# Seven-product second layers on 256-column blocks, one batch behind the first layers; first layers back to one level

## The chip, the cores and the metric

The kernel runs on one core of a Trainium2 chip. The metric is device time in microseconds (us): 1341.12 us, the median of three runs (1341.06 to 1343.45). "PE" is the matrix engine (TensorE), "PEld" its weight loads, "DVE" the vector engine, "ACT" the scalar engine, "POOL" GpSimd and "SP" the engine that issues the transfers.

## The reference, cut to what matters

Attention with a threshold mask gives `x` of 1152 tokens by 512. Two mixtures of experts follow, the first with 8 experts and gates from a normalisation, the second with 4 experts and given gates:

```
for e in range(E):
    h = np.maximum(x @ w1[e], 0.0)          # 1152x512 @ 512x1024
    out += P[:, e:e + 1] * (h @ w2[e])      # 1152x1024 @ 1024x512
```

Nearly all of the arithmetic is in these two matrix products per expert. All data are fp32.

## The kernel before

Every fp32 operand of a matmul is kept as two fp32r tiles, a high part (`hi`) and what it leaves over (`lo`), and a product is three passes: lo by hi, hi by lo and hi by hi. `split` (L70) makes the pair: ACT casts the high part (L72), POOL or DVE subtracts (L77).

Attention and part of experts 0 and 1 come first (up to some 330 us). Then follow 22 half experts, each with 512 of an expert's 1024 hidden columns (`halves`, L622): two of expert 0 with one batch of 576 tokens, twelve of experts 2 to 7, and eight of the second mixture. A batch is `c` = 0 or 1; 64 tokens of each are the "tail", which is gathered into a ninth token tile.

A first layer (`x @ w1`) of one batch is done in seven products for eight (Winograd's form of Strassen's method): tokens in two halves of 288, inputs and hidden columns in two halves, so that a product is 2 groups `g` of 6 matmuls with 288 columns (`layer1`, L929, 14 slots). The sums of weights are made on POOL, those of x beforehand. Sixteen of the 22 half experts, the set `TWO`, take both batches jointly and apply the same trick once more inside products 2 and 7 (`layer1_two`, L1049): 162 matmuls instead of 168.

A second layer (`layer2`, L1256) is plain: nine token tiles, each 4 hidden blocks by 3 passes by 512 output columns, so 108 matmuls. DVE then adds each tile times its gate to `acc` (L1284).

Each engine works its own list of instructions strictly in the order in which the program writes them. The weights of the next half expert are cooked (sum on POOL, cast on ACT, subtraction on POOL) from generators that `tick` (L763) advances between groups of matmuls, at most every second tick and `LAG` ticks after the sum they need. PSUM has 8 banks. After the last half expert of the first mixture (`turn`), `next_x` (L1201) turns the finished `acc` into the new x: PE transposes, ACT copies, and `pair` (L1243) makes the four sums and four splits on POOL.

Of the kernel before, what the change touches and what calls it, by code (L numbers as in the profile page):

```python
# [19 lines left out]
E1, E2 = 8, 4  # L20
# [10 lines left out]
def attention_two_moe_kernel(ctx, tc, qP, kP, qT, kT, vp, tau, wg, w1, w1s, w2, dp, m2w1s, m2w2, out):  # L31
# [495 lines left out]
    with ExitStack() as att:  # L527
# [76 lines left out]
        while raws:  # L604
# [11 lines left out]
    UNITS = (1, 2, 6, 7, 5, 3, 4)  # L616
    SLOTS = ((1, 0), (1, 1), (2, 0), (2, 1), (6, 0), (6, 1), (7, 0), (5, 0), (7, 1), (5, 1), (3, 0), (4, 0), (3, 1),
             (4, 1))
    HF = FT // 2
    ORDER = (2, 3, 0, 1)  # L620
    NB1, NB2 = 7, 5
    halves = [dict(w1=w1s, w2=w2, e=e, hf=h, chunks=(1,), p=p1) for e in (0,) for h in range(2)]  # L622
    halves += [dict(w1=w1s, w2=w2, e=e, hf=h, chunks=(0, 1), p=p1) for e in range(2, E1) for h in range(2)]
    turn = len(halves) - 1
    halves[turn]["chunks"] = (1, 0)
    halves += [dict(w1=m2w1s, w2=m2w2, e=e, hf=h, chunks=(0, 1), p=p2) for e in range(E2) for h in range(2)]
    halves[turn + 1]["chunks"] = (1, 0)
    TWO = {*range(3, turn), *range(turn + 3, len(halves))}
    base = [0]
    for i in range(len(halves)):  # L630
        base.append(base[-1] + (9 if i in TWO else 7))

    class Psum:
        def __init__(self):
            self.all = pool(ctx, "psum", 1, space=PSUM, reuse_waits="tile").tile([P, 8, 512], F32, name="mm")
            self.free, self.of = list(range(8)), {}

        def tile(self, *a, **kw):
            k = self.free.pop(0)
            t = self.all[:, k]  # L640
            self.of[id(t)] = t, (k,)
            return t
# [7 lines left out]

        def give(self, t):
            self.free.extend(self.of.pop(id(t))[1])

# [5 lines left out]
    shared = [xp.tile([P, 4608], F32, tag="shared", name="sums"), 0]  # L659

    def new_xy():
        if shared[0].dtype != F32:
            shared[0] = xp.tile([P, 4608], F32, tag="shared", name="sums")
# [8 lines left out]
    def cook1():  # L672


        def total(a, b, op):
            s = w1p.tile([P, DM], F32, tag="sum1", name="ws", bufs=3)
            G.tensor_tensor(s, a, b, op=op)
            return s, clock[0] + LAG

        for i, hv in enumerate(halves):  # L680
            a11, a12, a21, a22 = (w1p.tile([P, DM], F32, tag="raw1", name="raw", bufs=4) for _ in range(4))
            for k, a in enumerate((a11, a12, a21, a22)):
                nc.sync.dma_start(a, hv["w1"][hv["e"], hv["hf"], k])
            ready = clock[0] + LAND
            order = iter(range(base[i], base[i + 1]))

            def unit(src, at):
                yield next(order), at
                hi = w1p.tile([P, DM], F32R, tag="w1h", name="wh", bufs=NB1)
                lo = w1p.tile([P, DM], F32R, tag="w1l", name="wl", bufs=NB1)  # L690
                split(A, G, hi, lo, src)
                units[0].append((hi, lo))

            def within(src):
                x = w1p.tile([P, DM], F32, tag="sum1", name="wx", bufs=3)
                b = [src[:, k * P:(k + 1) * P] for k in range(4)]
                y = [x[:, k * P:(k + 1) * P] for k in range(4)]
                for k, (p, q, op) in enumerate(((b[2], b[3], ALU.add), (y[0], b[0], ALU.subtract),
                                                (b[0], b[2], ALU.subtract), (b[1], y[1], ALU.subtract))):
                    G.tensor_tensor(y[k], p, q, op=op)  # L700
                return x, clock[0] + LAG

            if i in TWO:
                yield 0, ready + LAG
                x2 = within(a12)
                yield from unit(a12, ready)
                yield from unit(*x2)
            yield 0, ready
            s1 = total(a21, a22, ALU.add)
            yield 0, ready  # L710
            s2 = total(s1[0], a11, ALU.subtract)
            yield from unit(a11, ready)
            if i not in TWO:
                yield from unit(a12, ready)
            yield 0, ready
            G.tensor_tensor(a21, a11, a21, op=ALU.subtract)  # L716
            s3 = a21, clock[0] + LAG
            yield 0, ready
            G.tensor_tensor(a12, a12, s2[0], op=ALU.subtract)
            s4 = a12, clock[0] + LAG  # L720
            if i in TWO:
                yield 0, ready
                x7 = within(a21)
                rest = s2, s1, s3, x7, s4
            else:
                rest = s2, s3, s1, s4
            for src in rest:
                yield from unit(*src)
            yield from unit(a22, ready)

    def cook2(w2p):
        raw = []
        todo2 = [(hv, k) for hv in halves for k in ORDER]
        for i in range(len(todo2)):
            while len(raw) < 3 and todo2:
                hv, k = todo2.pop(0)
                raw.append((w2p.tile([P, DM], F32, tag="raw2", name="raw", bufs=3), clock[0] + LAND))
                nc.sync.dma_start(raw[-1][0], hv["w2"][hv["e"], :, hv["hf"] * HF + k])
            yield i, raw[0][1]
            hi = w2p.tile([P, DM], F32R, tag="w2h", name="wh", bufs=NB2)  # L740
            lo = w2p.tile([P, DM], F32R, tag="w2l", name="wl", bufs=NB2)
            split(A, G, hi, lo, raw.pop(0)[0])
            units[1].append((hi, lo))

    cooks, heads = [cook1(), None], [None, None]
    heads[0] = next(cooks[0])

    def advance(k):
        heads[k] = next(cooks[k], None)

    def may(k):
        if cooks[k] is None or heads[k] is None:
            return False
        return heads[k][0] < freed[k] + (NB1, NB2)[k] and clock[0] >= heads[k][1]
# [8 lines left out]
    def tick(n=1):  # L763

        clock[0] += 1
        first = [k for k in (0, 1) if heads[k] is not None and clock[0] >= last[0] + PACE]
        first.sort(key=lambda k: 2 * (bisect(base, len(units[0])) - 1 if k == 0 else len(units[1]) // HF) + k)
        for k in first:
            if may(k):
                advance(k)  # L770
                last[0] = clock[0]
                break
        for _ in range(n):
            while behind and next(behind[0], None) is None:
                behind.pop(0)

    def need(k, u):
        while len(units[k]) <= u:
            advance(k)
        return units[k][u]  # L780


    def gate():
        lt = shared[0][:2 * E1, 12 * HS:]
# [48 lines left out]
        give(norms)  # L833
        yield 1
# [72 lines left out]
    w2p = pool(ctx, "w2", reuse_waits="tile")  # L907
    cooks[1] = cook2(w2p)
    advance(1)
# [17 lines left out]
    turned = []  # L927

    def layer1(i, c):  # L929
# [3 lines left out]
        last = c == hv["chunks"][-1]  # L933
        side = [[hp.tile([P, HF, HS], F32R, tag=f"h{s}{k}", name="hs") for k in "hl"] for s in "lr"]
        tail = hv.setdefault("tail", None) or [hp.tile([P, HF, P], F32R, tag=f"t{k}", name="ht") for k in "hl"]
        hv["tail"] = tail
        hv.setdefault("side", {})[c] = side
# [7 lines left out]
        def done(src, s, k, to=None):  # L945

            hh, hl = (side[s][j][:, k] for j in range(2))
            A.activation(hh, src, AF.Relu)
            V.scalar_tensor_tensor(hl, src, 0.0, f(hh), op0=ALU.max, op1=ALU.subtract)  # L949
            if to is not None:  # L950
                give(to)

        def rest(s):

            q = (2 * c + s) * 32
            for j in range(2):
                G.tensor_scalar(tail[j][:, :, q:q + 32], f(side[s][j][:, :, 2 * P:]), 1.0, 1.0,  # L957
                                op0=ALU.mult, op1=ALU.mult)

        st, late = [{}, {}], [[], []]  # L960
        kept = {}
        for u, g in SLOTS:
            if u == 6 and not g:
                drain(i, c)
            if u == 2 and turned:
                next_x(turned.pop(0))
# [4 lines left out]
            if first:  # L971
                z[b] = bank()
# [397 lines left out]
```

## Time and profile before

| what | value |
|---|---|
| median of three runs | 1341.12 us |
| the profiled execution's own time | 1342.76 us |
| its span, first to last instruction | 1340.6 us |
| busy share of the span: PE, PEld, DVE, ACT, POOL | 98%, 86%, 53%, 45%, 59% |
| the chain that ended last, by engine | PE 86%, DVE 6%, ACT 4%, POOL 3% |
| its largest lines | L1276 39%, L1073 25%, L976 6% |

Matmuls overlap: one of 512 columns is shown as 0.39 us long, but the next starts some 0.23 us after it. What one costs is the distance from start to start. The mean duration of a group is not that distance.

### The profile page before, as it was taken

What the parts mean: (1) busy time and instruction counts of PE and PEld (TensorE: products, weight loads), DVE (VectorE), ACT (ScalarE), POOL (GpSimd) and SP (SyncE); (2) the same over time, 40 slices, a digit from 0 to 9 for tenths busy, and PEclk for the clock granted to TensorE, in tenths of its full rate; (3) what the DMA queues carried; (4) which work ended last, traced back from release to release, by engine and by line L of the source; (5) the groups of instructions that cost most, each with busy time, mean ns of one, the idle gap of its engine ahead of it and who ended that gap; (6) DMA issues with size and microseconds to landing.
All of it is one profiled execution on the core that took longest, in us unless ns stands there. A gap on an engine that the chain in (4) does not pass through costs nothing.

```text
span 1340.6 us, 20707 instructions
## 1 busy us (share of the span) xinstructions
PE 1310.9 (98%) x7681; PEld 1155.1 (86%) x7681; DVE 706.3 (53%) x1478; ACT 601.6 (45%) x1220; POOL 790.3 (59%) x997
## 2 busy tenths in 40 slices
PE   7998999999999999999999999999899999999998
PEld 4597988889888998899899889989789989988997
DVE  5799988356885443443444344344336344434434
ACT  6887786322443443343244334325534424433430
POOL 6886975342875646655564665554863656466540
PEclk9999999999999999999999999999999999999999
DMA  4542330010320221022022102211111201210202
GB/s 148 163 126 71 96 103 17 24 33 24 96 71 2 63 64 40 25 64 64 3 62 64 39 26 63 64 32 41 55 32 32 64 1 63 64 37 27 64 1 71
DMA packets 42052, 73.56 MB, mean 55 GB/s; under 512 B 5088, under 2 KB 10336, under 8 KB 41952
## 3 DMA queue, kind: packets, MB, share of 16 engines
q1 hardware_dynamic: 41664, 71.96, 18.1%
q8 instruction: 61, 1.00, 0.3%
q14 instruction: 39, 0.32, 0.1%
q10 hardware_dynamic: 288, 0.28, 0.1%
HBM read 69.86 MB, written 2.36 MB: 54 GB/s over the span
## 4 chain that ended last, share of the span: by engine, by line
PE 86%; DVE 6%; ACT 4%; POOL 3%; issue 1%; DMA 0%; POOLq 0%; DVEq 0%; ACTq 0%
PE mm L1276 39%; PE mm L1073 25%; PE mm L976 6%; PE mm L501 5%; PE mm L473 4%; PE sc L272 2%; PE pv L349 2%; DVE ex L296 1%; PE et L314 1%; DVE st L277 1%; ACT ex L292 1%; PE pv L358 1%; DVE etl L331 1%; PE pv L356 1%; ACT eth L321 0%
## 5 line engine op out<-in xcount | busy, mean ns | idle before, releaser
L77 POOL TENSOR_TENSOR wl<-raw,wh 128x512 fp32r<-128x512 f32 x198 | 257.6, 1308 | 380.9 <-ACT wh L72 374.3
L1276 PE MATMUL mm<-wh,hs 128*128 128x512 f32 x1344 | 433.7, 397 | 2.8 <-DVE hs L949 2.0
L1276 PEld LDWEIGHTS mm<-wh,hs 128*128 128x128 f32 x1344 | 252.3, 188 | 68.4 <-DVE hs L949 5.2
L1284 DVE SCALAR_TENSOR_TENSOR acc<-mm,p,acc 128x512 f32<-128x512 f32 x181 | 135.3, 749 | 271.6 <-PE mm L1276 271.5
L1276 PE MATMUL mm<-wl,hs 128*128 128x512 f32 x672 | 265.0, 394 | 0.0
L1276 PEld LDWEIGHTS mm<-wl,hs 128*128 128x128 f32 x672 | 126.3, 188 | 28.1
L72 ACT CAST wh<-raw 128x512 fp32r<-128x512 f32 x198 | 122.7, 624 | 38.3 <-POOL raw L716 24.2
L1109 ACT COPY A<-mm 128x288 f32<-128x288 f32 x32 | 12.9, 402 | 188.7 <-PE mm L1073 188.7
L1073 PE MATMUL mm<-xh,wl 128*128 128x288 f32 x432 | 96.5, 296 | 0.0
L1073 PE MATMUL mm<-xl,wh 128*128 128x288 f32 x432 | 96.4, 295 | 0.0
L1073 PE MATMUL mm<-xh,wh 128*128 128x288 f32 x432 | 96.2, 295 | 0.0
L1119 DVE SCALAR_TENSOR_TENSOR hs<-mm,hs 128x576 fp32r<-128x576 f32 x96 | 72.5, 755 | 33.7 <-ACT hs L1115 32.2
L1115 ACT ACTIVATE hs<-mm 128x576 fp32r<-128x576 f32 x96 | 62.5, 651 | 55.2 <-DVE mm L1112 48.8
L1073 PEld LDWEIGHTS mm<-xh,wl 128*128 128x128 f32 x432 | 70.8, 189 | 0.7
L1073 PEld LDWEIGHTS mm<-xl,wh 128*128 128x128 f32 x432 | 70.7, 189 | 0.8
L1073 PEld LDWEIGHTS mm<-xh,wh 128*128 128x128 f32 x432 | 71.0, 189 | 0.0
L306 POOL TENSOR_SCALAR ex<-ex,st 128x576 f32<-128x576 f32 x72 | 54.2, 753 | 26.5 <-DVE st L304 23.6
L1073 PE MATMUL mm<-xth,wl 128*128 128x288 f32 x304 | 69.0, 296 | 0.0
L1073 PE MATMUL mm<-xth,wh 128*128 128x288 f32 x304 | 68.9, 295 | 0.0
L1073 PE MATMUL mm<-xtl,wh 128*128 128x288 f32 x304 | 68.8, 295 | 0.0
L296 DVE SCALAR_TENSOR_TENSOR ex<-sc,st,ex 128x576 f32<-128x576 f32 x72 | 58.5, 813 | 14.8 <-ACT ex L292 10.8
L1276 PE MATMUL mm<-wh,ht 128*128 128x512 f32 x176 | 58.2, 392 | 1.8 <-POOL ht L957 1.8
(220 smaller groups left out, 2934.6 us busy)
## 6 DMA issues: line engine op xcount, KB each, us to landing
raw<-in_w SPq DMA_DIRECT2D x88, 256.0 KB, 3.0
raw<-in_w1s SPq DMA_DIRECT2D x56, 256.0 KB, 3.2
raw<-in_m2w1s SPq DMA_DIRECT2D x32, 256.0 KB, 2.8
raw<-in_m2w SPq DMA_DIRECT2D x32, 256.0 KB, 2.9
kr<-in_kT SPq DMA_DIRECT2D x22, 288.0 KB, 3.0
vr<-in_vp SPq DMA_DIRECT2D x24, 160.0 KB, 2.4
qr<-in_qT SPq DMA_DIRECT2D x8, 288.0 KB, 2.8
out_y<-acc SPq DMA_DIRECT2D x8, 256.0 KB, 2.0
```

The lines of the kernel that those rows point to most:

```text
L72: A.copy(hi, src)
L77: el.tensor_tensor(lo, src, f(hi), op=ALU.subtract)
L296: V.scalar_tensor_tensor(ex, u["sc"][:, :, :HS], st[:, 2:3], ex, op0=ALU.is_ge, op1=ALU.mult, accum_out=st[:, 3:4])
L306: G.tensor_scalar(exf, exf, st[:, 5:6], 1.0, op0=ALU.mult, op1=ALU.mult)
L473: T.matmul(ph[:, :n], lhsT=a[:, kt * P:(kt + 1) * P], rhs=x[:, kt, n0:n0 + n], start=i == 0 and kt == 0, stop=i == 2 and kt == KT - 1)
L501: T.matmul(py, lhsT=x, rhs=a, start=i == 0, stop=i == 3 * FT - 1)
L976: T.matmul(m, lhsT=w[:, (2 * g + kt) * P:(2 * g + kt + 1) * P], rhs=operand(u, kt, lo), start=first and j == 0, stop=j == len(ops) - 1, sk ...
L1073: T.matmul(m, lhsT=w, rhs=x, start=first and j == 0, stop=last and j == len(ops) - 1, skip_group_check=True)
L1115: A.activation(sides[c][s][0][:, k:k + 2], src, AF.Relu)
L1119: V.scalar_tensor_tensor(hl, src, 0.0, f(hh), op0=ALU.max, op1=ALU.subtract)
L1276: T.matmul(py, lhsT=hs[x][:, k, o:o + P], rhs=w, start=n == 0, stop=n == 3 * HF - 1)
L1284: V.scalar_tensor_tensor(acc[t], py, s, acc[t], op0=ALU.mult, op1=ALU.add)
```

## The change

- All first layers are done one batch at a time in seven products, in the order 1, 7, 6, 4, 5, 2, 3; `layer1_two` and the sums inside x (`within_x`) go.
- Nineteen second layers are also done in seven products, per batch: hidden columns in two halves, output columns in two halves of 256, tokens in two halves of 256. Each product is 2 slots of 6 matmuls with 256 columns. The tail tile is done in four plain pieces of 6. The three half experts in `PLAIN` keep the old form.
- The hidden values need sums of quadrants, each split into hi and lo, seven `places` per batch. `split_hidden` spreads that work over the next first layer: `push` makes one step of it per slot, `late(k)` holds a step until slot k of a first layer (k below 10), sum1, sum2 and sum4 are one DVE instruction each, `split_of` is an ACT cast and a DVE subtraction, and `mend` (ACT, then DVE) puts the difference of two quadrants into bank pair C; so the second layer of a batch runs after the first layer of the batch behind it. At `turn` and at the end the lag is closed.
- The weights are cooked from one list, `STEPS`, for both layers: per half expert 14 splits and 8 sums (before 9 + 4 splits, 4 sums and two sets of four small ones in a joint half expert).
- PSUM banks are handed out singly and in pairs; the second layer updates `acc` in 128x256 pieces, two per `quarter`.

```
-    UNITS = (1, 2, 6, 7, 5, 3, 4)
+    UNITS = (1, 7, 6, 4, 5, 2, 3)
+    PARTS = "22", "3", "2", "12", "1", "11", "4"
+    PLAIN = {0, 1, turn + 1}
-    LAND, LAG, PACE = 6, 4, 2
+    LAND, LAG, PACE = 8, 5, 2
...
+    STEPS = ((SUM, "s3", "a2", "a0", "a2", "-"), (SUM, "s2", "+", "a3", "s3", "-"), (UNIT, 0, "a0"),
+             (UNIT, 0, "s3", "s3"), (SUM, "s1", "a0", "s2", "a0", "+"), (UNIT, 0, "s2"), (UNIT, 0, "a3", "a3"),
+             (SUM, "s4", "s2", "a1", "s2", "-"), (UNIT, 0, "s1", "s1"), (UNIT, 0, "a1", "a1"),
+             (SUM, "t1", "+", "b3", "b2", "-"), (UNIT, 0, "s4", "s4"), (SUM, "t3", "b3", "b3", "b1", "-"),
+             (UNIT, 1, "b2", "b2"), (SUM, "t2", "+", "b1", "t1", "-"), (UNIT, 1, "t3", "t3"), (UNIT, 1, "t2"),
+             (UNIT, 1, "b0"), (SUM, "t4", "b0", "b0", "t2", "-", "t2"), (UNIT, 1, "t1", "t1"), (UNIT, 1, "t4", "t4"),
+             (UNIT, 1, "b1", "b1"))
...
+        k = max(len(agenda) - (0 if i - 1 in PLAIN else 2), 0)
+        agenda[k:k] = [(i, s) for s in steps[:2]]
+        agenda += [(i, s) for s in steps[2:]]
...
     def tick(n=1):
         clock[0] += 1
+        if agenda and clock[0] >= last[0] + (PACE if agenda[0][0] > 2 else 1) and ready_step():
+            advance()
+            last[0] = clock[0]
...
+    def slot(n=1):
+        for d in sorted((x for x in due if x[0] <= now[0]), key=lambda x: x[:2]):
+            due.remove(d)
+            d[2]()
+        push()
+        tick(n)
+        now[0] += 1
+        phase[1] += 1
...
     def layer1(i, c):
+        phase[:] = 1, 0
+        for n, u in enumerate(UNITS):
+            b = {7: "C", 4: "C", 2: "B"}.get(u, "A")
+            first = b not in ch
+            if first:
+                ch[b] = until(banks.pool.pair)
+            for g in range(2):
...
+                if g:
+                    m = wide(ch[b])
+                    if u in (1, 7, 6):
+                        v[u] = snap()
+                        A.copy(v[u], m)
+                    elif u == 4:
+                        V.tensor_tensor(m, v[6], m, op=ALU.add)
+                    if u == 4 and not plain:
+                        after(1, lambda m=m: A.activation(h21, m, AF.Relu))
+                    elif u == 5:
+                        h22 = ch["h22"] = v[7]
+                        V.tensor_tensor(h22, m, h22, op=ALU.add)
+                    if u == 5 and not plain:
+                        after(1, mend)
+                        after(2, lambda: whole(ch, "22", G, main(h22)))
+                    elif u == 2:
+                        V.tensor_tensor(m, v[1], m, op=ALU.add)
+                        work.append(split_hidden(ch))
+                slot()
...
+    def whole(ch, name, el, src):
+        hi, lo = ch["ops"][name] = until(place)
+        split(A, el, hi, lo, src)
+    def quadrant(ch, name, m, copy=None):
+        hi, lo = ch["ops"][name] = until(place)
+        A.activation(hi, main(m), AF.Relu)
+        if copy is not None:
+            A.activation(copy, main(m), AF.Relu)
+        A.activation(th, rest(m), AF.Relu)
+        V.scalar_tensor_tensor(lo, main(m), 0.0, f(hi), op0=ALU.max, op1=ALU.subtract)
+        V.scalar_tensor_tensor(tl, rest(m), 0.0, f(th), op0=ALU.max, op1=ALU.subtract)
...
+    def split_hidden(ch):
+        whole(ch, "3", V, main(ch["C"]))
+        order = ((upper_right, 0), (sum1, 1), (sum2, 2), (upper_left, 3), (lambda: split_of("1"), 5),
+                 (lambda: split_of("2"), 6), (sum4, 7), (lambda: split_of("4", 2), 9))
+        for step, k in order:
+            yield from late(k)
+            yield from step()
...
-    def layer2(i, c):
+    def layer2(ch):
+        for n, part_ in enumerate(PARTS):
+            if end and n == (i != turn):
+                tail_tile()
+            for k in range(2):
+                product(m[:, 256 * k:256 * k + 256], lambda j, kt: hi[j][:, kt, P * k:P * (k + 1)], 0, w,
+                        not k and part_ in ("22", "3", "12"))
+                if k:
+                    places.append(hi)
+                    if part_ in ("22", "2"):
+                        A.copy(v[part_], m)
+                    elif part_ == "12":
+                        V.tensor_tensor(BB, v["22"], BB, op=ALU.add)
+                        quarter(1, 0, BB, True)
+                    elif part_ == "11":
+                        V.tensor_tensor(CC, v["2"], CC, op=ALU.add)
+                        quarter(0, 0, CC, True)
...
+                if i == turn and turned and c == hv["chunks"][-1]:
+                    next_x(turned.pop(0))
+                slot(1 + (i == turn))
+        if i == turn:
+            turned.extend(4 * c + t for t in (2, 3, 0, 1))
...
+    for n, (i, c) in enumerate(chunks):
+        ch = layer1(i, c)
+        ready.append(ch)
+        while ready and (i in PLAIN or len(ready) > 1 or i == turn and c == 0):
+            (layer2_plain if i in PLAIN else layer2)(ready.pop(0))
+    for ch in ready:
+        layer2(ch)
```

## Rows read from the trace of the kernel before

**Rows 1.** The page: busy us (share of the span) and instructions of each engine.

```profile
PE 1310.9 (98%) x7681; PEld 1155.1 (86%) x7681; DVE 706.3 (53%) x1478; ACT 601.6 (45%) x1220; POOL 790.3 (59%) x997
```

**Rows 2.** Busy by stretch: length, PE, PEld, DVE, ACT, POOL (instructions), clock, DMA, GB/s.

```profile
600.00:700.00 100.00, 99.94 (x568) 88.67 (x567) 41.76 (x65) 37.71 (x69) 60.45 (x73) 1.00 0.15 43
800.00:900.00 100.00, 99.65 (x567) 88.43 (x566) 41.62 (x64) 35.71 (x66) 53.89 (x60) 1.00 0.19 53
900.00:1000.00 100.00, 94.85 (x563) 83.61 (x562) 41.35 (x81) 46.83 (x125) 66.50 (x84) 1.00 0.13 38
```

**Rows 3.** The chain in order of time: start us, us, what, instructions.

```profile
666.33 21.52 PE mm L1073 x162
...
687.88 25.36 PE mm L1276 x108
713.24 21.59 PE mm L1073 x162
```

**Rows 4.** PE in order of time, attention: start, us, line, op, tiles, shape.

```profile
134.93 0.63 PE L356 MATMUL pv<-etl,vhl 128*128 128x256 f32 x4
135.40 0.75 PE L358 MATMUL pv<-eth,vhl 128*128 128x256 f32 x5
135.99 0.27 PE L314 MATMUL et<-ident,ex 128*128 128x128 f32 x1
```

**Rows 5.** Weight loads by line: busy us, mean ns, idle before.

```profile
L1276 PEld LDWEIGHTS mm<-wh,hs 128*128 128x128 f32 x1344 | 252.3, 188 | 68.4 <-DVE hs L949 5.2 <-DVE hs L1119 4.5
```

**Rows 6.** DVE by line and shape: busy us, mean ns, idle before.

```profile
L1284 DVE SCALAR_TENSOR_TENSOR acc<-mm,p,acc 128x512 f32<-128x512 f32 x181 | 135.3, 749 | 271.6 <-PE mm L1276 271.5
L1112 DVE TENSOR_TENSOR mm<-s,mm 128x576 f32<-128x576 f32 x32 | 24.4, 762 | 23.1 <-ACT s L1109 19.9 <-PE mm L1073 2.6
L482 DVE SCALAR_TENSOR_TENSOR hl<-mm,hh 128x256 fp32r<-128x256 f32 x24 | 10.2, 424 | 8.1 <-ACT hh L479 6.3 <-issue 1.4
L1238 DVE TENSOR_TENSOR xl<-mm,xh 128x512 fp32r<-128x512 f32 x5 | 3.5, 692 | 9.1 <-ACT sums L1237 7.4 <-PE mm L976 1.7
```

**Rows 7.** ACT by line and shape.

```profile
L72 ACT CAST wh<-raw 128x512 fp32r<-128x512 f32 x198 | 122.7, 624 | 38.3 <-POOL raw L716 24.2 <-DMA raw<-in_w 7.4 <-DMA raw<-in_m2w 3.6
L1109 ACT COPY u<-mm 128x576 f32<-128x576 f32 x32 | 20.6, 644 | 0.0
L505 ACT COPY y<-mm 128x512 f32<-128x512 f32 x4 | 2.3, 586 | 9.2 <-PE mm L501 9.2
```

**Rows 8.** POOL by line and shape.

```profile
L77 POOL TENSOR_TENSOR wl<-raw,wh 128x512 fp32r<-128x512 f32 x198 | 257.6, 1308 | 380.9 <-ACT wh L72 374.3 <-PE mm L1073 6.2
L1131 POOL TENSOR_SCALAR ht<-hs 128x128 fp32r<-128x128 f32 x128 | 35.0, 303 | 16.7 <-ACT hs L1115 10.3 <-DVE hs L1119 6.4
```

**Rows 9.** PE, ACT and DVE in order of time, one joint half expert.

```profile
713.33 0.29 PE L1073 MATMUL mm<-xh,wh 128*128 128x288 f32 x1
713.66 0.40 ACT L1109 COPY A<-mm 128x288 f32<-128x288 f32 x1 [12.31 <-PE mm L1073]
713.96 0.62 ACT L72 CAST wh<-raw 128x512 fp32r<-128x512 f32 x1
714.12 0.46 DVE L1112 TENSOR_TENSOR mm<-A,mm 128x288 f32<-128x288 f32 x1
...
721.26 0.76 DVE L1112 TENSOR_TENSOR mm<-s,mm 128x576 f32<-128x576 f32 x1
721.93 0.75 DVE L1119 SCALAR_TENSOR_TENSOR hs<-mm,hs 128x576 fp32r<-128x576 f32 x1
```

**Rows 10.** Waits: engine, line, releaser; us in total, times, longest us.

```profile
ACT wh L72 <- POOL ws L677: 46.6, 14, 3.3
```

**Rows 11.** POOL in order of time, the turn: first and last of 16 `pair` instructions.

```profile
925.87 0.74 POOL L1244 TENSOR_TENSOR sums<-sums 128x256 f32<-128x256 f32 x1 [11.16 <-ACT sums L1237]
...
947.51 0.73 POOL L77 TENSOR_TENSOR xl<-sums,xh 128x256 fp32r<-128x256 f32 x1
```

**Rows 12.** PE and DVE in order of time, the end.

```profile
1336.44 0.40 PE L1276 MATMUL mm<-wh,hs 128*128 128x512 f32 x1
1336.88 0.75 DVE L1284 SCALAR_TENSOR_TENSOR acc<-mm,p,acc 128x512 f32<-128x512 f32 x1 [2.03 <-PE mm L1276]
```

More of the change, by code (lines that the diff above doesn't have):

```diff
@@ L635, in __init__ @@
             self.all = pool(ctx, "psum", 1, space=PSUM, reuse_waits="tile").tile([P, 8, 512], F32, name="mm")
[L636 to L642, printed above, removed]
+            self.free, self.of, self.kept = list(range(6)), {}, [6, 7]
         def take(self, *ks):
@@ L667, in attention_two_moe_kernel @@
     w1p = pool(ctx, "w1", side="right", reuse_waits="tile")
-    LAND, LAG, PACE = 6, 4, 2
+    hrp = pool(ctx, "hsr", side="right", reuse_waits="tile")
+    w2p = [None]
+    LAND, LAG, PACE = 8, 5, 2
     units, freed, clock, last = ([], []), [0, 0], [0], [0]
[L672 to L678, printed above, removed]
-        for i, hv in enumerate(halves):
[L681 to L754, printed above, removed]
+    free_raw = [w1p.tile([P, DM], F32, name=f"raw{k}") for k in range(5)]
+    free_sum = [w1p.tile([P, DM], F32, name=f"sum{k}") for k in range(2)]
+    def fetches():
+        for i, hv in enumerate(halves):
+            for k in (2, 0, 3, 1):
+                yield f"a{k}{i}", hv["w1"][hv["e"], hv["hf"], k]
+            for k in ORDER if i in PLAIN else (2, 3, 1, 0):
+                yield f"b{k}{i}", hv["w2k"][hv["e"], :, hv["hf"] * HF + k] if i in PLAIN else hv["w2"][hv["e"], hv["hf"], k]
@@ L833, in gate @@
         give(norms)
+        banks.pool.free.extend(banks.pool.kept)
         yield 1
@@ L925, in drain, with halves_of, snap, after @@
                 pending[c] = None
-    turned = []
+    def halves_of(t, at):
+        return [part(t, at + 512 * j, 2, 2 * P) for j in range(2)]
+    places = [halves_of(pl.tile([P, 1024], F32R, name=f"h{k}"), 0) for k, pl in enumerate((hp, hp, hp, hrp))]
+    places += [halves_of(tails, 1024), halves_of(tails, 2048)]
+    tail = [hp.tile([P, HF, P], F32R, name=f"tail{k}") for k in "hl"]
+    owner = [None]
+    turned, held, now, due, work = [], {}, [0], [], []
+    hurry, phase = [False], [0, 0]
+    def snap(n=HS):
+        return tp.tile([P, 2, HS], F32, tag="snap", name="snap", bufs=7)[:, :, :n]
+    def after(k, op):
+        due.append((now[0] + k, len(due), op))
+    def push():
+        if work and next(work[0], None) is None:
+            work.pop(0)
+    def slot(n=1):
[6 more added lines that the diff above has]
+        phase[1] += 1
+    def until(get):
+        while (t := get()) is None:
+            assert work
+            hurry[0] = True
+            push()
+        hurry[0] = False
+        return t
+    def wide(t):
+        return t[:, :, :HS]
+    def main(t):
+        return t[:, :, :2 * P]
+    def rest(t):
+        return t[:, :, 2 * P:HS]
     def layer1(i, c):
@@ L932, in layer1 @@
         L, R = slice(c * S, c * S + HS), slice(c * S + HS, c * S + S)
[L933 to L937, printed above, removed]
+        end = c == hv["chunks"][-1]
+        plain = i in PLAIN
+        ch = dict(i=i, c=c, ops={}, soon=(i, c) in ((turn, 0), (len(halves) - 1, 1)))
         def operand(u, kt, lo):
@@ L943, in operand @@
             return x[:, kt + 2 * (u in (2, 3)), R if u in (3, 5) else L]
[L945 to L958, printed above, removed]
@@ new lines, in earlier_ends, with update @@
+    def earlier_ends(i):
+        hv = halves[i]
+        for j in range(2):
+            G.tensor_scalar(tail[j][:, :, :64], f(tail0[hv["e"]][j][:, hv["hf"] * HF:(hv["hf"] + 1) * HF]), 1.0, 1.0,
+                            op0=ALU.mult, op1=ALU.mult)
+        if hv["hf"]:
+            places.append(halves_of(tails, 0))
+    fresh = set()
+    def update(hv, t, cols, src):
+        a, e = acc[t][:, cols], hv["e"]
+        s = hv["p"][:, t, e:e + 1]
+        if len(src.shape) == 3:
+            a = a.rearrange("p (a b) -> p a b", a=2)
+        if hv["p"] is p2 and e == 0 and hv["hf"] == 0 and (t, cols.start) not in fresh:
+            fresh.add((t, cols.start))
+            V.tensor_scalar(a, src, s, None, op0=ALU.mult)
+        else:
+            V.scalar_tensor_tensor(a, src, s, a, op0=ALU.mult, op1=ALU.add)
@@ new lines, in layer2_plain @@
+    def layer2_plain(ch):
+        i, c = ch["i"], ch["c"]
+        hv = halves[i]
+        end = c == hv["chunks"][-1]
+        phase[:] = 2, 0
+        if i < 2:
+            earlier_ends(i)
+        ts = [4 * c, 4 * c + 1, 4 * c + 2, 4 * c + 3] + [8] * end
+        for t in ts:
+            py = until(banks.pool.single)
+            n = 0
+            for j, k in enumerate(ORDER):
+                w = need(1, base2[i] + j)
+                hid = tail if t == 8 else ch["ops"]["21"[k < 2] + "12"[t % 4 // 2]]
+                kk, o = (k, 0) if t == 8 else (k % 2, P * (t % 2))
+                for x, y in ((0, 1), (0, 0), (1, 0)):
+                    T.matmul(py, lhsT=hid[x][:, kk, o:o + P], rhs=w[y], start=n == 0, stop=n == 3 * HF - 1)
+                    n += 1
+                if t == 8:
+                    freed[1] += 1
+                slot()
+            update(hv, t, slice(0, DM), py)
+            banks.pool.give(py)
+            if turned:
+                next_x(turned.pop(0))
+        places.extend(ch["ops"].values())
@@ L1298, in start_within @@
[L1298 to L1315 removed]
+                    nc.sync.dma_start(out[HS * q + 2 * P:HS * (q + 1), :], acc[8][32 * q:32 * (q + 1)])
```

536 lines of the change are left out of this document (247 added, 289 removed).

## The prediction

> **What bounds the kernel now.** I read the page's engine line first, then the busy time by stretch, then the chain of waits in order of time, and then durations by line and shape. PE is busy 98% of the span, no other engine above 59%, leaving weight loads aside [rows 1]; in a steady stretch PE is busy 99.94 of 100 us and DMA 15% [rows 2]. The chain shows what it is busy with: in a joint half expert 162 matmuls of 288 columns in 21.5 us, then 108 of 512 columns in 25.4 us, with nothing between [rows 3]. So the kernel's length there is a sum of matmul distances, and what the change is worth is first what it does to that sum, and then what PE has to wait for that it did not wait for before.
>
> **Prices on PE.** From start to start a matmul costs 21.55 / 162 = 133 ns with 288 columns and 25.36 / 108 = 234.8 ns with 512 [rows 3]. The new shape, 256 columns on 128x128 weights, is in the attention stage: nine of them between 134.93 and 135.99, each with its own weights, so 1.06 / 9 = 118 ns [rows 4]. Scaled by columns the other two shapes give 118 (288) and 117 (512); the three agree, and I take 118, with 117 to 120 for the range.
>
> A rule of the Trainium skill speaks against the change here. A load of 128x128 weights is shown as 188 ns long [rows 5]. "TensorE: Matmul & The Clock Gate", section "Part 3", under "What overlaps and what doesn't", says that a weight load overlaps a running matmul only when the two use different row groups. All these loads use the whole array. If so, no matmul here could follow the last by less than load and stream together, and halving the columns would double the part that loads cost. Nine loads and nine matmuls in 1.06 us contradict it: 118 ns is less than one load as shown. By the rule a 256-column product could not come under 188 ns, which is the rival "loads" below.
>
> **The sum on PE.** Per half expert not in PLAIN, of which there are 19, the second layer goes from 108 x 234.8 ns = 25.36 us to 2 x 84 + 24 = 192 matmuls x 118 = 22.66 us: 2.70 us less, 51.3 us in all. Seven products for eight saves one eighth, and the four pieces of the tail tile keep their old cost; the rest is that 118 is a hair over half of 234.8. The first layer goes from 162 to 168 matmuls in the 16 joint half experts: 16 x 6 x 133 ns = 12.8 us more. Net 38.5 us less. Half experts 0, 1 and 14 keep their matmuls. A steady half expert takes 22.3 + 22.7 = 45.0 us for 46.9.
>
> **Do the other engines keep up on average?** Per half expert, by durations of [rows 6 to 8] (a 64-wide piece estimated at 0.22 us, a 256-wide update with a gate at 0.49, from 0.424 and the 0.06 by which the gated 512 is above the plain one):
> DVE per batch: 3 adds of 576 (0.76), 10 operations of 512 (0.69), 2 narrow, then 2 adds of 512 and 10 updates of 256: 2.3 + 6.9 + 0.4 + 1.4 + 4.9 = 15.9; twice, and 1.5 for the tail: 33 us of 45, 74%.
> ACT per batch: 5 of 576 (0.65), 10 of 512 (0.59 to 0.62), 2 narrow: 9.7; twice, and 14 casts at 0.62: 28 us, 62%.
> POOL: 14 subtractions, 8 sums and 2 splits of h22 at 1.31, and 1.9 of narrow work for the tail: 33 us, 74%.
> None passes PE. The transfers stay 8 of 256 KB per half expert, at 15% of DMA [rows 2], issued by SP as buffers are dropped.
>
> **Where PE can wait: product 3.** On average is not enough, since the queues are in order. The tightest place is product 3 of a first layer: it adds into bank pair A, which DVE's add for product 5 must have read. That add stands on DVE behind this list of the earlier batch's work: subtraction for sum 1, subtraction for sum 2, add of product 4, sum 4; and the first of these waits for an ACT cast behind the copies of products 7 and 6. Slots are 6 x 133 = 0.80 us. What the neighbouring rows give: a result can be read 0.20 us after the next matmul's start would fall (713.33 + 0.29, read at 713.66, against 713.47 for the distance), DVE starts 0.06 after ACT's end, and an independent next instruction starts about 0.09 to 0.10 before its predecessor's end on DVE and on ACT [rows 9]. From the first layer's start: copy of 7 from 3.39 to 4.03; two relus of the upper left quadrant to 4.62; copy of 6 from 4.99 to 5.63; cast of sum 1 to 6.11; DVE from 6.17: subtraction to 6.86, the second to 7.46, add of 4 to 8.13, sum 4 to 8.73, add of 5 to 9.40, so A is free at 9.46. Product 3 starts at 12 x 0.798 = 9.58. It just does not wait.
> By STEPS and the places freed, weights are cooked on every second slot through the second batch's first layer and hardly in the first batch's. Two casts of 0.62 then stand between: the cast of sum 2 ends at 7.13, the add of 5 at 9.82, and product 3 waits 0.3 us. 19 x 0.3 = 6 us, which I take. Bounds: 0 if no cast falls there; with every duration counted whole and no overlap, 0.35 for a first batch and 1.34 for a second, 19 x 1.7 = 32 us.
> In the second layer the tight place is part "4", which reuses the bank that DVE updates from after part "1": parts are 1.41 us apart, DVE has add 0.69 and four updates 0.49 in 2.83 us, so it ends about 0.1 us early; 0, at most 0.2 x 38 = 8 us. The other hidden work has a whole layer, some 10 us, until it is read: nothing.
>
> **The turn.** PE sits idle 5.1 us in its stretch now [rows 2]. There the lag is closed: the last two second layers of the first mixture follow each other, so the new x of batch 1 is made beside one second layer instead of beside a first and a second one. POOL's sixteen instructions for it take from 925.87 to 948.24, 22.4 us, weights cooked between them [rows 11]; of their own they are 16 x 0.73 = 11.7. From the third transposed tile to product 7 of the next first layer there are about 10 us: the second layer with tail and transposes 14.9, minus 6.3 before that tile, plus two slots. PE waits 2 to 12 us, and up to 6 more for the ninth tile. I take 9, between the ends, since POOL still has weights to cook. Behind PE's waiting matmul stands all of its work, so this is paid in full.
>
> **The end.** Now: the last matmul starts at 1336.44, DVE follows with 0.75 [rows 12], then the output goes. After: two updates of 256, each with its own transfer. The same within 0.3 us; for the last batch, whose hidden sums squeeze into one second layer, 1 us.
>
> **The sum.** 1342.76 (the profiled execution's own time) - 38.5 + 6 + 9 + 1 = 1320.3. That execution is 1.6 us over the median of the runs, so the time is 1318.6; I say 1318.
>
> **Rivals.**
> "Clean": the turn's chain is hidden as it is now and no cast gets in the way: 1341.1 - 38.5 = 1302.6. For it: PE waits next to nothing now [rows 2]. Against: the turn has lost half its cover. Chance 0.12.
> "Whole durations": ACT and DVE lose their overlap, since nearly every operation in the list now waits for the other engine. 32 in place of 6 gives 1344.6, about no change. For it: half of the steps in the list do wait for another engine. Against: the adds and sums do not depend on each other. Chance 0.09, spread over 1335 to 1350.
> "Sums late" (slower): a weight cast on ACT waits for its POOL sum, with the PSUM copies queued behind it, and PE behind them. Now ACT waits 14 times, 46.6 us in all, 3.3 us each, for one kind of sum [rows 10], at no cost because PE's copies have longer to go; POOL's load rises from 60% [rows 2] to 74%. One such wait per half expert in the second batch's first layer is 19 x 3.3 = 63 us: 1381. It decides from 22.5 / 19 = 1.2 us per half expert. Against: the cast now follows its sum by 5 slots at least, mostly by 8, over 6 us, while POOL needs 1.3 per step. Chance 0.09.
> "Loads": a 256-column matmul costs the 188 ns of its load [rows 5]: 19 x 192 x 0.07 = 255 us more, 1574. Rows 4 speak against it. Chance 0.01.
>
> **How the numbers follow.** My forecast has 0.69, and its own range is 1306 to 1334 (no waits but a short turn; the turn at 18 us and half of the bound at product 3). The range to 8 in 10 is 1302 to 1341: below it 0.05, above it 0.15 ("sums late", "loads", part of "whole durations"). About 0.2%, 2.7 us, is what a measurement can tell from no change. Faster by more: 0.69 + 0.12 + 0.03 of "whole durations" = 0.84. Within: 0.03. Slower: 0.09 + 0.01 + 0.03 = 0.13.
>
> **What would show it.** A chain with pieces of 192 matmuls in about 22.7 us and 168 in 22.3; matmuls of 256 columns 118 ns apart (at 130 ns 44 us of the gain is gone, and the forecast falls). PE's idle time should be named at product 3, released by DVE's add of product 5, some 0.3 us in every second batch, and at the turn, released by POOL's splits. DVE and POOL near 74% and ACT near 62% in a steady stretch, PE above 98%. If PE is below 96% there, the queues' order and not the matmuls decide, and the prediction is wrong.

## The result and the profile after

The changed kernel takes 1320.91 us, the median of four runs (1320.25 to 1321.72), against 1341.17 us (1341.06 to 1343.45) for the kernel before on the same chip. The ratio is 0.9845, with a 95% interval of 0.9828 to 0.9862: faster by 1.55%. The forecast was 1318 us with a range of 1302 to 1341. The profiled execution took 1321.72 us against 1342.76 before, 21.0 us less; the account below explains that difference.

The page's engine line of the kernel after answers to [rows 1]:

```profile
PE 1279.3 (97%) x9373; PEld 1217.6 (92%) x9373; DVE 886.4 (67%) x1875; ACT 739.6 (56%) x1459; POOL 904.2 (69%) x992
```

PE has 1692 more matmuls, narrower ones, and is busy for 32 us less; DVE works 180 us more, ACT 138, POOL 114. The busy time by stretch, with the columns of [rows 2]:

```profile
300.00:400.00 100.00, 93.29 (x526) 83.10 (x525) 68.98 (x131) 38.12 (x83) 63.83 (x76) 0.97 0.16 48
600.00:700.00 100.00, 100.00 (x805) 99.86 (x804) 67.04 (x127) 54.60 (x105) 75.27 (x77) 1.00 0.18 53
...
900.00:1000.00 100.00, 90.09 (x589) 82.89 (x588) 49.48 (x89) 49.24 (x117) 72.45 (x81) 0.95 0.15 43
```

In steady stretches PE does not wait at all. Behind the attention it waits mainly at two places: the first half experts (300 to 400, called the start below) and the turn (900 to 1000). The chain of waits of a steady stretch of the kernel after, with the columns of [rows 3]:

```profile
650.02 11.20 PE mm L1013 x84
661.22 12.64 PE mm L1289 x108
673.86 11.17 PE mm L1013 x84
685.03 9.83 PE mm L1289 x84
```

First layers (L1013) and second layers (L1289) alternate by batch with nothing between. The two second layers hold 108 and 84 matmuls, 12.64 + 9.83 = 22.47 us; the mean of the 15 steady half experts (425 to 886 and 1032 to 1257) is 22.61 us, so 22.61 / 192 = 117.8 ns from start to start. A first layer has 11.2 / 84 = 133 ns. A half expert takes 45.0 us, as the forecast had it. (The expectation of x1 below has 22.55 us for the second layers; the trace gives 22.61.)

PE's two longest waits in the kernel after (line and tile, releaser: us in total, times, longest):

```profile
PE mm L1013 <- ACT xth L71: 5.9, 1, 5.9
PE mm L1013 <- DVE snap L1030: 5.3, 1, 5.3
```

The 5.9 is in the turn, the 5.3 in the start, each once. The account of the profiled difference, each stage read from PE's first matmul to its last in both traces ("lost beside the matmuls" is the stage's length less its matmuls at the distances above):

| stage | forecast | measured | how |
|---|---|---|---|
| second layers of 19 half experts | -51.3 | -52.3 | 19 x (25.36 - 22.61) |
| first layers of 16 half experts | +12.8 | +13.1 | 16 x (22.37 - 21.55) |
| product 3, steady | +6 | 0 | PE busy 100.00 of 100 us |
| the start | no term | +8.5 | lost beside the matmuls: 10.7 after, 2.2 before |
| the turn | +9 | +8.7 | lost beside the matmuls: 16.5 after, 7.8 before |
| the end | +1 | +1.2 | last 192 matmuls 23.80 in place of 22.61 |
| sum | -22.5 | -20.8 | profiled: -21.0 |

What remains, 0.2 us, is not accounted for.

### The profile page after: what moved, and what is told of

It is laid out like the page before. It is cut to its first block, busy times and chain, and to the rows that moved or that the text cites. A ratio compares the mean times of both kernels' runs of the same rounds, so it can differ in the third digit from the quotient of the medians.

```text
span 1319.9 us, 25049 instructions
## 1 busy us (share of the span) xinstructions
PE 1279.3 (97%) x9373; PEld 1217.6 (92%) x9373; DVE 886.4 (67%) x1875; ACT 739.6 (56%) x1459; POOL 904.2 (69%) x992
## 4 chain that ended last, share of the span: by engine, by line
PE 65%; DVE 2%; POOL 1%; ACT 1%; issue 0%; DVEq 0%; POOLq 0%; ACTq 0%
PE mm L1013 33%; PE mm L1289 31%; PE mm L1119 2%; DVE acc L1100 1%; POOL wl L76 0%; POOL xtl L76 0%; DVE h L1075 0%; ACT h L1071 0%; ACT sums L1243 0%; ACT wh L71 0%; DVE more L1075 0%; DVE tails L1075 0%; ACT snap L1073 0%; POOL sums L1252 0%; DVE taill L1076 0%
## 5 line engine op out<-in xcount | busy, mean ns | idle before, releaser
L1100 DVE SCALAR_TENSOR_TENSOR acc<-mm,p,acc 128x256 f32<-128x256 f32 (+1 forms) x428 | 195.3, 508 | 66.7 <-PE mm L1289 63.3
L1289 PE MATMUL mm<-wh,h 128*128 128x256 f32 x960 | 177.2, 283 | 0.0
L1020 ACT COPY snap<-mm 128x576 f32<-128x576 f32 x126 | 80.8, 642 | 151.9 <-PE mm L1013 106.5
L1013 PE MATMUL mm<-xh,wl 128*128 128x288 f32 x672 | 146.2, 299 | 5.3 <-DVE snap L1030 5.3
L1289 PEld LDWEIGHTS mm<-wh,h 128*128 128x128 f32 x960 | 149.6, 191 | 0.0
L1013 PE MATMUL mm<-xh,wh 128*128 128x288 f32 x672 | 144.2, 296 | 0.0
L1013 PE MATMUL mm<-xl,wh 128*128 128x288 f32 x672 | 144.1, 296 | 0.0
L1289 PE MATMUL mm<-wl,h 128*128 128x256 f32 x480 | 136.9, 285 | 3.3 <-ACT snap L1331 1.9
L1289 PE MATMUL mm<-wh,tails 128*128 128x256 f32 x696 | 124.3, 278 | 0.0
L1013 PE MATMUL mm<-xth,wl 128*128 128x288 f32 x504 | 109.4, 298 | 8.3 <-ACT xth L71 5.9
L76 POOL TENSOR_TENSOR wl<-sum,wh 128x512 fp32r<-128x512 f32 x82 | 107.6, 1313 | 11.4 <-ACT wh L71 11.4
L1013 PEld LDWEIGHTS mm<-xh,wl 128*128 128x128 f32 x672 | 107.4, 189 | 7.3 <-issue 5.5
L1013 PE MATMUL mm<-xtl,wh 128*128 128x288 f32 x504 | 108.8, 297 | 0.1
L1013 PEld LDWEIGHTS mm<-xh,wh 128*128 128x128 f32 x672 | 108.5, 190 | 0.0
L1013 PEld LDWEIGHTS mm<-xl,wh 128*128 128x128 f32 x672 | 108.5, 190 | 0.0
L1013 PE MATMUL mm<-xth,wh 128*128 128x288 f32 x504 | 108.3, 296 | 0.0
L1289 PEld LDWEIGHTS mm<-wh,tails 128*128 128x128 f32 x696 | 105.7, 188 | 0.0
L1289 PE MATMUL mm<-wl,tails 128*128 128x256 f32 x348 | 97.0, 279 | 0.0
L1289 PEld LDWEIGHTS mm<-wl,h 128*128 128x128 f32 x480 | 91.6, 191 | 4.0 <-ACT snap L1331 2.1
```

The costliest lines, as they stand in the source:

```text
L76: el.tensor_tensor(lo, src, f(hi), op=ALU.subtract)
L1013: T.matmul(ch[b][:, g, :HS], lhsT=w[:, (2 * g + kt) * P:(2 * g + kt + 1) * P], rhs=operand(u, kt, lo), start=first and j == 0, stop=j == l ...
L1020: A.copy(v[u], m)
L1100: V.scalar_tensor_tensor(a, src, s, a, op0=ALU.mult, op1=ALU.add)
L1289: T.matmul(m, lhsT=hid(x, kt + ko), rhs=wk[y], start=first and n == 0, stop=n == 5, skip_group_check=True)
```

## The experiments

All runs stand beside runs of the kernel before on the same chip in the same session: 1342.73 us for the first four, 1343.03 us for the next three, 1341.33 us for the last two. The first four kernels were timed once.

### The second layers plain again

**x1.** All 22 half experts are put in `PLAIN`: second layers of 512 columns, no lag, and one-level first layers. The rest of the edit hands every half expert the plain weights and keeps the turn and the output going. Here and in x2 the ninth tile is turned last, so products 1 and 7 of the first half expert after the turn take the tail tokens' x from before the turn. The instructions are the same, but PE's wait of 5.9 us for that tile does not occur in either trace.

```
-    PLAIN = {0, 1, turn + 1}
+    PLAIN = set(range(len(halves)))
...
```

> All second layers in the old form of 108 matmuls with 512 columns, no lag; first layers at one level as in the changed kernel. Theory (the gain is the matmul sum of the second layers, 25.36 against 22.55 us per half expert, 19 of them): 54 us over the changed kernel's profiled 1321.7, less up to 9 for a turn as before, plus up to 20 for the waits at the joint between layers: 1365 to 1390. Rival (the gain comes from one-level first layers and the new order of the work, and the halved columns bring nothing): at most 1330.

1382.04 us, as the theory had it and far from the rival: the first layers alone make the kernel slower, and the seven-product second layer is what gains. The chain of the kernel x1, columns as above:

```profile
607.02 6.39 PE mm L1013 x48
...
621.00 12.23 PE mm L1119 x52
...
644.66 11.18 PE mm L1119 x48
655.84 6.40 PE mm L1013 x48
```

A half expert takes 655.84 - 607.02 = 48.82 us, where 168 x 133 ns + 108 x 234.8 ns = 47.7: without the lag 1.1 us of DVE's and ACT's work on the last products shows per half expert, 0.7 in the second layer of one batch (14.79 us for 60 matmuls, which are 14.1) and the rest in the two first layers. So the lag has a worth of its own, beside the seven products. It does not carry the result: 19 x 1.1 = 21 us less, an estimate, would still leave x1 at 1361 us, above the kernel before.

**x2.** The seven products stay, the lag goes: the second layer of a batch runs right behind its own first layer, with the tail tile at its end.

```
-        while ready and (i in PLAIN or len(ready) > 1 or i == turn and c == 0):
+        while ready and (i in PLAIN or len(ready) > 0 or i == turn and c == 0):
...
```

> The second layer of a batch directly behind its own first layer, with the tail tile at its end; same instructions otherwise. Theory (the lag hides the splitting of the hidden sums, some 10 operations of 0.6 to 0.7 us in a chain between ACT and DVE): PE waits 3 to 6 us in each of 38 batches, 1435 to 1550, waits named at the second layer's matmuls, released by DVE's subtractions. Rival (the queues catch up in a second layer whose first parts are ready early): under 1340.

1782.44 us: the rival is out, but the loss, 461 us, is well over the expectation's. PE's waits in the kernel x2 (columns as above), its page's engine line, and the busy time from 600 to 800 us:

```profile
PE mm L1289 <- ACT h L71: 117.5, 36, 5.8
PE mm L1289 <- ACT tails L71: 74.2, 23, 4.5
PE mm L1289 <- ACT more L71: 48.1, 15, 3.4
```

```profile
PE 1468.0 (82%) x9373; PEld 1368.3 (77%) x9373; DVE 900.8 (51%) x1875; ACT 748.0 (42%) x1459; POOL 901.9 (51%) x992
```

```profile
600.00:800.00 200.00, 158.57 (x1036) 152.64 (x1036) 87.47 (x158) 73.97 (x138) 90.72 (x91) 0.87 0.11 31
```

The waits for the casts of the hidden sums are the three lines, 239.8 us, and with the other waits at L1289 some 280. The rest is in PE's busy time: the same 9373 matmuls are shown busy for 1468.0 us, 189 more than the 1279.3 of the kernel after. The clock goes with it: its mean is 0.87 in this stretch, where it is 1.00 in the kernel after, and a matmul costs more in the slower parts (last section). The expectation had priced the waits and left out the clock; how much of the 189 us is the clock alone was not measured.

### How much room product 3 has

**x3, x4.** Is the chain on DVE hidden with room to spare, or at the edge? One (x3) or two (x4) repeats of the 512-wide subtraction for sum 2 are put into DVE's list, 0.69 us each. They write the same values again.

```
+            if name == "2":
+                for _ in range(1):          # x4: range(2)
+                    hi, lo = ch["ops"]["2"]
+                    V.tensor_tensor(lo, b["2"], f(hi), op=ALU.subtract)
```

> One more DVE subtraction per batch, the same again, behind the one for sum 2 (start to start 0.6 us). Theory (in-order queue): in the trace of the changed kernel DVE's add of product 5 ends 9.25 us after the start of the first layer, and product 3 is due at 9.57, so 0.3 us are free and the rest, 0.3 us, is paid in each of 38 batches: 1333 (1327 to 1340), wait named at the first layer's matmul, released by that add. Rival (average load): DVE goes from 67 to 70 percent busy and PE does not notice: 1322.

> Two more of them per batch. Theory (in-order queue): 0.9 us paid per batch, 35 us, 1356 (1348 to 1366). Rival (average load): DVE at 73 percent, 1322.

1347.39 and 1374.58 us: 25.7 and 52.9 us over the profiled execution of the kernel after, for 38 batches 0.68 and 1.39 us each on average. The rival, that DVE has room because it is busy 67% of the time, is out: one instruction of 0.69 us in a list with a third of its time free costs its whole length. The chain of one first layer of the kernel x3, short pieces left out:

```profile
656.44 4.76 PE mm L1013 x36
...
661.27 0.65 ACT snap L1020
661.92 0.49 ACT h L71
...
662.43 1.30 DVE h L76 x2
...
663.75 0.69 DVE h L1171
664.45 0.67 DVE mm L1022
665.12 0.60 DVE mm L1193
665.72 0.67 DVE snap L1030
...
666.52 1.84 PE mm L1013 x12
```

This is the forecast's list, instruction for instruction, with the repeat (L1171) in it: copy of 6, cast, two subtractions, repeat, add of 4, sum 4, add of 5, product 3. Both sizes were missed, since the expectations allowed for 0.3 us free and counted 0.6 for a repeat; the repeat waits for the end of the subtraction before it and takes 0.7, and next to nothing is free. (The expectation's 9.25 us for the end of the add of product 5 is a misreading: in the trace of the kernel after it ends 9.37 to 9.43 us after the first layer begins.)

### The two places where PE waits

**x5.** The turn's sixteen splits go from POOL to DVE.

```
         for t, (hi, lo) in zip((t2, x12, x21, x11), to):
-            split(A, G, hi, lo, t)
+            split(A, V, hi, lo, t)
```

> At the turn the four subtractions of each pair are made by DVE in place of POOL. Theory (PE waits there for POOL's chain, 5.9 us at product 7 of the next first layer, and is slow at a lowered clock behind it): POOL's chain loses some 7 us, PE's wait falls below 2 us, 1313 (1310 to 1317). Rival (the chain is bound by the transposes, the ACT copies and the order of issue, or DVE's work then delays the second layer's updates): 1320 to 1323.

1316.44 us (1315.92 to 1317.71), ratio to before 0.9805 [0.979, 0.9819]. The wait of 5.9 us is gone, and another has come, at a second layer that waits for a bank that DVE's updates of `acc` have to read. PE in order of time in the kernel x5 (start, us, line, op, tiles, shape, idle before and its releaser):

```profile
939.38 0.58 PE L1289 MATMUL mm<-wl,more 128*128 128x256 f32 x1 [2.87 <-DVE acc L1100]
```

The turn (the six batches around it) goes from 157.2 to 153.2 us. A further 1.5 us of the difference lies before the edit does anything, since this execution's first half expert starts at 329.89 us and that of the kernel after at 331.43; it is not a gain of the edit. The granted clock from 20 to 40 us is 1.00 here and 0.91 in the kernel after, in code that is the same; x7, x8 and x9 below have the same 1.5 us.

**x6.** While a first layer of the start runs, DVE's sums of x make no step; they are made beside second layers, one in every slot from the fourteenth on.

```
-        for _ in g:
+        for k, _ in enumerate(g):
             yield 1
-            while phase[0] == 1 and phase[1] % 2:
+            while phase[0] == 1:
                 yield 1
-            if phase[0] == 2 and phase[1] % 2:
+            if phase[0] == 2 and phase[1] % 2 and k < 13:
                 yield 1
```

> The sums of x for the other batch, which DVE makes at the start, are not issued during the first layer of half expert 1, and the last of them faster in the second layers. Theory (these adds, 1.0 to 1.5 us each beside POOL against 0.45 alone, stand ahead of DVE's adds of products 4 and 5, and PE waits 5.3 us at product 3): that wait goes, of 7 us 2 come back at the next first layer, where the rest is drained: 1316 (1313 to 1319). Rival (the work only moves, and PE waits as long at the drain): 1320 to 1323.

1318.96 us (1318.17 to 1318.98), ratio 0.9821 [0.9806, 0.9835], which overlaps the interval of the kernel after; the timing alone does not settle it. The stage does: from the start's first layer to the fifth one it takes 89.48 us for 93.39, and the wait of 5.3 us is gone. Less than that wait is gained, because two short ones are new. PE of the kernel x6:

```profile
372.58 0.47 PE L1119 MATMUL mm<-wl,more 128*128 128x512 f32 x1 [1.11 <-ACT tailh L1074]
...
388.75 0.40 PE L1013 MATMUL mm<-xtl,wh 128*128 128x288 f32 x1 [1.05 <-DVE xtl L76]
```

**x7.** Both edits, x5 and x6.

> Both edits together. Theory: the two waits are apart and their gains add, 1308 (1303 to 1313). Rival: 1320 to 1323.

1316.71 us (1315.31 to 1318.85), ratio 0.9811 [0.9794, 0.9827]: no better than x5. The start takes 90.97 us and the turn 154.73, each 1.5 more than where the edit stands alone. In both stages the granted clock has it. In the start x6 and x7 have the same waits, but after the one of 0.79 us before product 6 of a first layer x7 has half the clock. The next fifteen matmul records, in x6 and then in x7 (columns of [rows 2]):

```profile
391.00:392.94 1.94, 1.94 (x15) 1.94 (x15) 1.92 (x3) 0.55 (x2) 1.86 (x3) 1.00 0.37 125
```

```profile
389.50:392.94 3.44, 3.44 (x15) 3.44 (x15) 1.94 (x3) 0.64 (x2) 3.36 (x4) 0.52 0.21 76
```

That is the 1.5 us of the start. In the turn PE comes to the wait for DVE's updates sooner than in x5, so it shows as 4.39 us in place of 2.87, and behind it the clock stays at half for 5.05 us in place of 2.92. Why the clock falls in one execution and not in the other was not found.

**x8, x9.** In x8 the turn's splits alternate between DVE and POOL; x9 is x8 with the edit of x6.

```
-        for t, (hi, lo) in zip((t2, x12, x21, x11), to):
-            split(A, G, hi, lo, t)
+        for k, (t, (hi, lo)) in enumerate(zip((t2, x12, x21, x11), to)):
+            split(A, (V, G)[k % 2], hi, lo, t)
```

> At the turn DVE makes two of each four subtractions (sums t2 and x21), POOL the other two. Theory (two queues share one chain): with all four on DVE, POOL's wait at product 7 went but a new one of 2.9 us came at the second layer's matmul, released by DVE's update of acc; with half of them the new one stays under 1 us and POOL's chain is some 4 us shorter than with none: 1316 (1313 to 1319). Rival (whichever queue has the rest makes PE wait the same): 1319 to 1322.

> The same with the quiet first layer of half expert 1. Theory: the edits lie at two places some 550 us apart, so their gains add: 4 us less than x8_turn_shared, 1312 (1309 to 1316). Rival (as when all four were on DVE: no gain over the one edit): 1316 to 1318.

x8: 1317.07 us (1316.61 to 1318.08), ratio 0.9817 [0.9802, 0.9832]. x9: 1313.99 us (1312.87 to 1314.9), ratio 0.9793 [0.9777, 0.981]. The turn takes 153.78 and 153.22 us, the start of x9 91.01, with the same half clock as in x7. The expectation that the wait behind DVE's updates falls below 1 us was wrong: 3.4 us stay in x8, 3.5 in x9. The interval of x9 lies wholly under that of the kernel after: it has the lowest median here, 27.3 us under the kernel before in its own session, 1.5 of them before any edit of it acts. PE's waits in the kernel x9 from 300 us on:

```profile
PE mm L1289 <- DVE acc L1100: 4.9, 3, 3.5
...
PE mm L1013 <- ACT xth L71: 0.4, 1, 0.4
```

## Why the prediction was right

**The price of a matmul.** This is the step that carries the result, and it held: 118 ns forecast for 256 columns, 117.8 measured, 133 and 133 for 288. With the measured distances the net on PE is -39.2 us for -38.5. The price came from nine matmuls of another stage [rows 4], and x1 shows that the gain is the second layer's. The rule of the Trainium skill that the prediction weighed ("TensorE: Matmul & The Clock Gate", section "Part 3") does not describe these matmuls: each has its own weights, a load of them is shown as 191 ns on average, and PE still starts one every 117.8 ns. PEld is busy 99.86 us of 100 in the stretch from 600 to 700; that looks like the bound, but the 22.61 us are what the columns cost: 234.8 / 512 = 0.459 ns a column in the old second layer, where PEld was busy 88.67 us of 100 [rows 2], and 117.8 / 256 = 0.460 in the new one.

**The other engines' load.** Forecast 74%, 62% and 74% for DVE, ACT and POOL in a steady stretch; measured 67%, 55% and 75% from 600 to 700, and for POOL 68% to 75% over the steady stretches. The forecast added up whole durations, while successive instructions of DVE and ACT overlap (679.27 + 0.59 lies past 679.75 below); that this makes the whole difference is not shown. "Sums late" did not happen. ACT's wait for POOL's sums, [rows 10] before, did rise in the kernel after:

```profile
ACT wh L71 <- POOL sum L752: 68.9, 21, 3.9
```

None of it reached PE in the steady stretches, where PE was busy 100.00 of 100 us.

**Product 3.** The list was right, the choice between its two ends was not. By hand the add of product 5 ends 9.40 us after the first layer begins; in the trace it ends 9.37 to 9.43 after. The forecast then took 9.82, with a weight cast between the casts of the hidden sums, hence 6 us. In the second batch of the half expert shown above, the kernel after has on ACT, DVE and PE:

```profile
679.27 0.59 ACT L71 CAST h<-mm 128x512 fp32r<-128x512 f32 x1
679.75 0.61 ACT L71 CAST more<-mm 128x512 fp32r<-128x512 f32 x1
680.23 0.64 ACT L71 CAST wh<-raw 128x512 fp32r<-128x512 f32 x1
```

```profile
679.90 0.69 DVE L76 TENSOR_TENSOR h<-mm,h 128x512 fp32r<-128x512 f32 x1 [0.70 <-ACT h L71]
680.51 0.68 DVE L76 TENSOR_TENSOR more<-mm,more 128x512 fp32r<-128x512 f32 x1
681.10 0.75 DVE L1022 TENSOR_TENSOR mm<-snap,mm 128x576 f32<-128x576 f32 x1
681.76 0.69 DVE L1189 TENSOR_TENSOR mm<-snap,mm 128x512 f32<-128x512 f32 x1
682.36 0.75 DVE L1030 TENSOR_TENSOR snap<-mm,snap 128x576 f32<-128x576 f32 x1
```

```profile
683.27 0.43 PE L1013 MATMUL mm<-xh,wl 128*128 128x288 f32 x2
```

There is a weight cast (680.23), but it stands behind the two casts of the sums, not between them, and DVE runs its five instructions end to end. The add of 5 ends at 682.36 + 0.75 = 683.11, and product 3 starts at 683.27, at its own pace: some 0.1 us to spare. x3 and x4 show from the other side how thin that is. Six of the forecast's us were for a place where nothing was lost, and nothing stood against a place where 8.5 were.

**The start.** This term was missing. DVE makes the sums of x for the later half experts while the first ones run; the prediction says of the half experts 0 and 1 only that they keep their matmuls. In the kernel before that stage lost 2.2 us beside its matmuls, in the kernel after 10.7. DVE of the kernel after, then PE:

```profile
364.29 1.54 DVE L870 TENSOR_TENSOR sums<-sums 128x288 f32<-128x288 f32 x1
...
368.68 1.51 DVE L875 TENSOR_TENSOR sums<-sums 128x288 f32<-128x288 f32 x1
370.11 0.75 DVE L1022 TENSOR_TENSOR mm<-snap,mm 128x576 f32<-128x576 f32 x1
...
372.38 0.75 DVE L1030 TENSOR_TENSOR snap<-mm,snap 128x576 f32<-128x576 f32 x1
```

```profile
373.27 0.82 PE L1013 MATMUL mm<-xh,wl 128*128 128x288 f32 x2 [5.29 <-DVE snap L1030]
```

Four sums, of which the first and the last are shown, 6 us in all, stand ahead of the adds of products 4 and 5 (L1022, L1030), so product 3 waits 5.29 us: the very place that the prediction worked out for the steady stretch, at a time that it did not look at. x6 takes the sums out of the first layer and the wait goes; the stage gets 3.9 us shorter, so a part of the 8.5 stays.

**The turn.** Forecast 9 us between bounds of 2 and 18, measured 8.7. The place, product 7 behind POOL's pairs and splits, and the reason, half the cover gone, both held; but what comes last is the ninth tile, whose cost the forecast had only as an addition of up to 6 us to its bound. That the sizes agree is luck in part: the wait at that place is 5.92 us and not 9, and the rest of the 8.7 is half a clock behind waits (last section) and short waits elsewhere, for which the forecast had no term. PE in the turn, and POOL's work for that tile (the first of its four sums, and the first splits):

```profile
947.16 0.85 PE L1013 MATMUL mm<-xth,wl 128*128 128x288 f32 x2 [5.92 <-ACT xth L71]
```

```profile
945.38 0.46 POOL L1250 TENSOR_TENSOR sums<-sums 128x128 f32<-128x128 f32 x1
...
947.15 1.29 POOL L76 TENSOR_TENSOR xtl<-sums,xth 128x128 fp32r<-128x128 f32 x3
```

x5 and x8 relieve POOL and the wait goes, but 2.9 to 3.4 us return at the second layer before it, since DVE then has the work ahead of its updates.

So the total came out within 3 us of the forecast partly by compensation: 6 us too many at product 3, 8.5 too few at the start, 0.7 too little gained on PE. One bound of the prediction's own inner range does not follow from its words: with the turn at 18 us and half of 32 us at product 3 its sum gives 1337.6 us and not 1334. Nothing else was worked out from it.

## What to carry to other kernels

Price a changed matmul by its distance from start to start, taken from any stage that has the shape, and ask of the rest whether an in-order list meets its deadline, not whether an engine is busy: at 67% load the list on DVE had 0.1 us to spare, and one instruction more per batch cost 25.7 us. Walk such a list through every stage in which other work shares the engine, the first and the last above all; where the steady stretch has no room, whatever else is queued there lands in full on the engine that waits. And give hidden work a whole stage of lag: in x2 the same products without it cost 461 us, part of it through the clock.

## What the hardware showed that was not expected

**DVE beside POOL.** The DVE additions with both inputs in SBUF (128x288) vary by a factor of three. The line's instructions in the kernel after, duration in ns as min, median and max:

```profile
L866 DVE TENSOR_TENSOR sums<-xh,xl x16: 448/693/1546, 274.5 to 363.5; 128x288 f32<-128x288 f32 x16
```

The long ones lie beside POOL's subtractions and sums. Here are a short one, with POOL idle, and a long one with POOL's subtraction beside it:

```profile
274.49 0.45 DVE L866 TENSOR_TENSOR sums<-xh,xl 128x288 f32<-128x288 f32 x1
...
350.77 1.50 POOL L76 TENSOR_TENSOR wl<-sum,wh 128x512 fp32r<-128x512 f32 x1
351.05 1.55 DVE L866 TENSOR_TENSOR sums<-xh,xl 128x288 f32<-128x288 f32 x1
```

DVE's 512-wide subtractions with one input in PSUM keep their 0.68 to 0.69 us in the steady stretch above, where POOL is busy 75%. The Trainium skill, "SBUF — State Buffer", section "Who interferes with whom", says that a DVE instruction with two SBUF inputs contends with a GpSimd instruction that reads SBUF, and that one with at most one SBUF input does not, outside the modes that use two ports; the trace agrees with both halves in the main. One exception is in view: the sum at 281.09 takes 0.50 us although POOL is shown busy with a subtraction. No run changed POOL's work beside these sums alone, so the cause is read from the trace and not shown by an experiment. The prediction missed the start partly because it had no such row: it priced DVE by the lines with an input in PSUM.

**The clock after a wait.** PE's granted clock by stretch in the kernel after, around the two longest waits (columns of [rows 2]):

```profile
941.00:943.80 2.80, 0.24 (x2) 0.01 (x1) 0.00 (x0) 0.94 (x3) 2.80 (x4) 1.00 0.36 94
944.00:950.60 6.60, 3.37 (x12) 3.02 (x13) 0.00 (x0) 1.63 (x5) 6.00 (x12) 0.50 0.01 1
...
373.27:376.29 3.02, 3.02 (x12) 3.02 (x13) 2.46 (x4) 0.99 (x3) 1.43 (x2) 0.50 0.30 90
```

PE stops at 941.2, is granted half its clock (1.2 of 2.4 GHz) from 944 to 950.6, and still has it when it resumes at 947.16; the same follows the wait that ends at 373.27. So each of the two waits costs something behind it as well. At the start PE's twelve matmuls of 288 columns from 373.27 take until 376.29, 3.02 us in place of 12 x 0.133 = 1.60. At the turn the twelve from 947.16 take until 950.64, 3.48 us, but there a part is POOL again, whose second split releases PE at 948.08. This is a part of why the start lost 8.5 us more than before while the wait named there is 5.3; the rest of that difference was not taken apart.
